# Attention and two MoE layers on one core: engine orders from block 6 on, staged weight preparation, weight loads at the turn

## The chip, the cores and the metric

The kernel runs on one core of one Trainium2 chip. The metric is the device time of one execution in microseconds (us). Before the change the median of three runs is 1075.56 us.

## The reference, cut to what matters

```python
def _attn_ref(q, k, v, f):                       # 4 batches, 8 heads, 576 tokens, head size 64
    cum = np.cumsum(np.log(np.clip(f, 0.0001, 1.0)), axis=-1)
    scores = q @ k.transpose(0, 1, 3, 2) / np.sqrt(64) + cum[:, :, :, None] - cum[:, :, None, :]
    ...                                          # causal mask, softmax
    return attn @ v

def reference(...):                              # x: 2304 tokens x 512
    h = np.maximum(x @ w_in, 0.0)                # first MoE layer, 512 -> 2048
    x = h * h @ w_out                            # 2048 -> 512
    h = x @ w_in2                                # second MoE layer
    return (h - np.tanh(h)) @ w_out2
```

All matmuls keep close to float32 exactness: each operand is held as a rounded half ("hi", h) and a rest ("lo", l), and a product is three matmuls: hi x hi, lo x hi, hi x lo. The weights of the second layer, w2, come as 64-bit numbers.

## The kernel before

**Blocks 0 to 7.** The first layer goes over 8 blocks of 288 tokens (TB), each in 16 steps i. `h_step` makes 12 matmuls (L157) into the one PSUM bank "h"; ScalarE makes ReLU (L161), the rounded square gh (L162) and the square (L163) from it, and VectorE the rest gl = square - gh (L117, the helper `rest`). `y_step` of the same step comes two steps later (LAG = 2): 12 matmuls (L173), of which those with gl need VectorE. The next h step can only start when ReLU has read the bank. The attention of the tokens lies beside blocks 0 to 5.

**Preparation for the second layer.** It lies beside blocks 6 and 7. w2 is cut in 8 pieces g for each half s (s = 0: w_in2, s = 1: w_out2); nine are prepared here: (0, 0) to (0, 7) and (1, 0). A piece means: `prep_fetch` reads raw 64-bit numbers; twice `prep_wide` (ScalarE, L765, tile wx), `prep_shift` (VectorE, L773) and `prep_or` (VectorE, L780) make 32-bit floats in tile wt; four `prep_sum` (VectorE, L785) build the sums of weights that a Strassen-like product of 7 factors needs; four casts `prep_hi` (ScalarE, L104) and four rests `prep_lo` (GpSimd, L117) split them; `prep_store` writes the piece to memory, and `w_load` reads it again when its place is free. Pieces in the table DIRECT are made in place instead. `PREPS` says after which (block, step) a piece is issued. The inputs x of the second layer are prepared in the same way for each of four quarters of the tokens: `x_load`, four sums `x_sum` (VectorE, L866), and `x_op` (cast on ScalarE L104, rest on GpSimd L117).

**Second part.** 32 steps n: quarter b, piece g. Each has 7 products of 6 matmuls (L969): P6, P1, P7 and P5 of step n, then P2, P4 and P3 of step n - 1, in a ring of 7 PSUM banks. ScalarE copies (L1103, L1108) and VectorE sums (L1104, L1107, L1120, L1121) combine them; tanh (L975) and the subtractions (VectorE L976, GpSimd L1132) give g = h - tanh(h), which `h_store` (L981) writes to g_d. Beside these steps the x operands of the next quarter and the pieces (1, 1) to (1, 7) are prepared (`PREP2_AT`: first step of a piece, which then takes four steps).

**The turn and the last part.** The last part has 32 product steps of 42 matmuls with 256 columns (L1045) and 192 matmuls more in `y_rest` (L1057). Its operands: `y_load` reads a g tile (L1008), `y_sum` makes four sums (VectorE, L1020), `y_hi` casts (ScalarE L104, tile go) and `y_lo` makes the rest (VectorE L117, tile go). Its weights are read by `w_load` into the places of w_in2 as those come free (`YLOAD_AT`, `HOME_G`); all DMAs go through the one queue of SyncE (SP), in order. "The turn" is the stretch around the last steps of the second part and the first of the last part.

**What sets the order.** The program is built twice. Up to step MARK, (2, 0), each engine follows the order of the first build. From there to the end of block 7 a scheduler that simulates a timeline orders the instructions. From the point where `second_part` is noted, before the change behind `part1.close()`, each engine's order is that in which the code emits its instructions:

```python
    for chain in ([by_name[n] for n in order if n in first_part], [x for x in emitted if x.name not in second_part]):
```

## Time and profile before

| | |
|---|---|
| median of three runs | 1075.56 us (1072.48 to 1077.96) |
| profiled execution, whole | 1073.96 us |
| its span | 1072.2 us |
| mean granted clock of TensorE | 0.987 |
| TensorE busy | 994.2 us, 93% |
| VectorE busy | 756.4 us, 71% |
| ScalarE busy | 586.1 us, 55% |
| GpSimd busy | 405.5 us, 38% |

The profile is of one execution. Its span goes from the first to the last instruction and is 1.76 us shorter than that execution's device time. Engines: PE is TensorE's matmuls, DVE is VectorE, ACT is ScalarE, POOL is GpSimd, SP is SyncE. L157 is line 157 of the kernel. "out<-in" are the program's names of tiles, "x12" a number of instructions. A wait is shown as the idle time of an engine with what ended it. Chain means the chain of work that ended last, followed back from the last instruction.

### The profile page before, as it was taken

The page shows a single profiled execution, that of the slowest core. Times are in us where ns is not written, and L with a number is a line of the kernel's source. Part 1 is how long each engine was busy: PE and PEld are TensorE (multiplying, and loading weights), DVE is VectorE, ACT ScalarE, POOL GpSimd, SP SyncE. Part 2 cuts the span into 40 slices and gives each one's busy share as a digit, 9 for nine tenths or more (in the row PEclk, how much of TensorE's full clock was granted, in tenths as well). Part 3 has the DMA queues.
Part 4 walks back from the last instruction along what each step waited for, and adds up shares of the span by engine and source line. Part 5 has one row for each costly group of instructions (what it writes and reads, how often), then busy time and mean ns, then how long its engine had stood idle before and what let it go on. Part 6 is the DMA issues. An engine that isn't in the chain of part 4 may idle for free.

```text
span 1072.2 us, 19736 instructions
## 1 busy us (share of the span) xinstructions
PE 994.2 (93%) x7008; PEld 925.1 (86%) x7008; DVE 756.4 (71%) x1843; ACT 586.1 (55%) x1314; POOL 405.5 (38%) x484
## 2 busy tenths in 40 slices
PE   4989999999999898998989998999999979999998
PEld 3676678888888788887889998999999979999998
DVE  5897777777777686787523766468877778777761
ACT  6887777765555455454435675446565644333330
POOL 4254455564454443543211556127576440000000
PEclk9899999999999999899999999999999999999999
DMA  7667642225864657744534994696867697335352
GB/s 239 196 151 206 193 141 98 89 86 174 273 196 158 191 176 219 251 130 132 194 120 145 318 335 141 224 417 230 320 244 269 259 346 266 135 98 175 121 163 74
DMA packets 86738, 211.55 MB, mean 197 GB/s; under 512 B 8592, under 2 KB 33232, under 8 KB 84336
## 3 DMA queue, kind: packets, MB, share of 16 engines
q1 hardware_dynamic: 86640, 210.29, 59.4%
q8 instruction: 55, 0.90, 0.3%
q14 instruction: 43, 0.35, 0.1%
HBM read 132.21 MB, written 78.05 MB: 196 GB/s over the span
## 4 chain that ended last, share of the span: by engine, by line
PE 58%; DMA 16%; DVE 14%; ACT 4%; issue 4%; POOL 2%; SPq 2%; POOLq 0%; DVEq 0%; ACTq 0%
PE wp L1045 15%; PE wp L969 13%; PE hp L157 9%; PE yp L173 8%; DMA PTl<-p_d 7%; PE o_ps L559 3%; DMA raw<-in_w_dram 3%; DMA p_d<-T 2%; PE wp L1057 2%; DVE PTl L117 2%; PE o_ps L374 2%; SPq L525 1%; DMA R<-in_qk_dram 1%; DVE P L450 1%; DVE gl L117 1%
## 5 line engine op out<-in xcount | busy, mean ns | idle before, releaser
L157 PE MATMUL hp<-xhl,w 128*128 128x288 f32 x1536 | 238.2, 301 | 7.1 <-ACT tmp L161 6.2
L157 PEld LDWEIGHTS hp<-xhl,w 128*128 128x128 f32 x1536 | 216.9, 192 | 13.6 <-ACT tmp L161 8.0
L173 PE MATMUL yp<-gh,w 128*128 128x288 f32 x1024 | 183.7, 299 | 0.5 <-ACT tmp L161 0.5
L969 PE MATMUL wp<-xo,wg 128*128 128x288 f32 x1152 | 162.4, 298 | 6.5 <-DMA wg<-wg_d 2.4
L1045 PE MATMUL wp<-go,wg 128*128 128x256 f32 x1344 | 162.7, 283 | 4.3 <-DVE go L117 3.3
L1045 PEld LDWEIGHTS wp<-go,wg 128*128 128x128 f32 x1344 | 161.7, 192 | 5.3 <-DVE go L117 4.1
L969 PEld LDWEIGHTS wp<-xo,wg 128*128 128x128 f32 x1152 | 156.9, 190 | 8.7 <-DVE gq L976 2.9
L173 PEld LDWEIGHTS yp<-gh,w 128*128 128x128 f32 x1024 | 153.9, 190 | 1.9 <-ACT tmp L161 0.7
L173 PE MATMUL yp<-gl,w 128*128 128x288 f32 x512 | 116.7, 301 | 12.1 <-DVE gl L117 9.3
L161 ACT ACTIVATE tmp<-hp 128x288 f32<-128x288 f32 x128 | 51.8, 405 | 123.8 <-PE hp L157 118.9
L104 ACT ACTIVATE go<-gt 128x1792 fp32r<-128x1792 f32 (+1 forms) x34 | 58.3, 1717 | 108.0 <-PE wp L1045 62.0
L459 ACT ACTIVATE P<-P,ST 128x320 f32<-128x320 f32 (+4 forms) x151 | 84.5, 561 | 43.1 <-DVE ST L450 42.2
L117 DVE TENSOR_TENSOR gl<-tmp,gh 128x288 fp32r<-128x288 f32 x96 | 58.4, 608 | 62.7 <-ACT tmp L163 62.3
L173 PEld LDWEIGHTS yp<-gl,w 128*128 128x128 f32 x512 | 84.0, 189 | 16.8 <-DVE gl L117 13.1
L470 POOL TENSOR_SCALAR P<-P,ST 128x448 f32<-128x448 f32 (+4 forms) x88 | 59.3, 676 | 96.9 <-DVE ST L464 54.8
L117 DVE TENSOR_TENSOR go<-gt,go 128x1792 fp32r<-128x1792 f32 (+1 forms) x34 | 69.3, 2038 | 27.6 <-ACT go L104 24.3
L117 POOL TENSOR_TENSOR wt<-wt,whi 128x512 f32<-128x512 f32 (+1 forms) x48 | 63.9, 1352 | 61.3 <-ACT whi L104 50.4
L117 DVE TENSOR_TENSOR PTl<-PTl,PTh 128x512 fp32r<-128x512 f32 (+1 forms) x64 | 51.7, 839 | 41.3 <-POOL PTh L106 41.3
L450 DVE CUSTOM_DVE_ANT_0 P<-s_ps,mk 128x320 f32<-128x320 f32 (+3 forms) x151 | 63.2, 433 | 25.1 <-PE s_ps L484 14.8
L106 POOL TENSOR_SCALAR PTh<-PTl 128x512 fp32r<-128x512 f32 (+1 forms) x64 | 46.1, 747 | 51.8 <-DMA PTl<-p_d 51.7
L1132 POOL TENSOR_TENSOR gq<-sm,sm 128x288 f32<-128x288 f32 x31 | 26.9, 868 | 94.1 <-ACT sm L1131 87.3
L1020 DVE TENSOR_TENSOR gt<-gt 128x256 f32<-128x256 f32 x128 | 53.4, 458 | 9.4 <-DMA gt<-g_d 8.3
(158 smaller groups left out, 1771.8 us busy)
## 6 DMA issues: line engine op xcount, KB each, us to landing
raw<-in_w_dram SPq DMA_DIRECT2D x64, 512.0 KB
wg<-wg_d SPq DMA_DIRECT2D x24, 896.0 KB
g_d<-gq SPq DMA_DIRECT2D x32, 576.0 KB
p_d<-T SPq DMA_DIRECT2D x16, 1024.0 KB
PTl<-p_d SPq DMA_DIRECT2D x64, 256.0 KB
gt<-g_d SPq DMA_DIRECT2D x32, 512.0 KB
R<-in_qk_dram SPq DMA_DIRECT2D x24, 576.0 KB
xhl<-x_d SPq DMA_DIRECT2D x14, 576.0 KB
```

Of the source, the lines that this page charges most:

```text
L104: eng.activation(out, in_, AF.Copy)
L106: eng.tensor_scalar(out, in_, 1.0, 1.0, ALU.mult, ALU.mult)
L117: eng.tensor_tensor(out, in_, hi.bitcast(F32), ALU.subtract)
L157: nc.tensor.matmul(ps, w[:, k * 128:(k + 1) * 128], x[:, k], start=(jj == 0), stop=(jj == 11))
L161: nc.scalar.activation(tmp, ps, AF.Relu)
L173: nc.tensor.matmul(yp[m][:, :n], w[:, c], x, start=(at == 0 and j == 0), stop=(at == NF - 1 and j == 2))
L450: nc.vector.tensor_tensor_reduce(p[:rows, a:b], ps[:rows, :b - a], mk[:rows, o:o + b - a], -0.125, 3.0e38 if mn is None else mn, ALU.add, ...
L459: nc.scalar.activation(p[:rows, :n], p[:rows, :n], AF.Exp, bias=mn, scale=-1.0, accum_out=st[:rows, 1, t:t + 1])
L470: by(n_by).tensor_scalar(p[:rows, :n], p[:rows, :n], st[:rows, 3, t:t + 1], 1.0, ALU.mult, ALU.mult)
L969: nc.tensor.matmul(ps, wg[:, ws, k * 128:(k + 1) * 128], xo[:, xs, k], start=(i == 0 and first_), stop=(i == 5), skip_group_check=True)
L1020: nc.vector.tensor_tensor(o, x, y, ALU.subtract)
L1045: nc.tensor.matmul(ps, wg[:, ws, m * 128:(m + 1) * 128], YO[n][xs][:, YX[xn]], start=(j == 0 and m == 0 and i == 0), stop=(j == 2 and i == ...
```

## The change

Four things are changed. (1) `second_part` is noted at the start of block 6, so that in blocks 6 and 7 too each engine follows the order of emission. (2) In these blocks a piece of w2 starts every third step (`PREPS` now counts the 32 steps of blocks 6 and 7) and is done in steps of its own: wide, shifts and ORs in the first, four sums and half of the casts and rests in the second, the other half in the third, the stores in the fourth (`prep_step`, `beside`); raw numbers are fetched two pieces ahead into two buffers; sums and operands of x stand at fixed steps (`XSUM_AT`, `XOP0_AT`); x of block 7 is read at step 8 of block 6 instead of 13. (3) In the second part three x sums stand in step 5 of a quarter and one in step 7, the pieces of w_out2 take the steps of `PREP2` (the last two earlier than before), and of the weights of the last part two pieces are loaded behind steps 27 and 30 and four behind the first four product steps, with `HOME_G` changed to suit. (4) At the turn g tiles are read behind other steps (`YGT_AT`), `y_sum(0)` stands a step earlier, `y_lo(0)` too, `y_hi(1)` ahead of the last P2; at the end the second half of `y_rest` finishes one output half before it starts the other.

```diff
-PREPS = (((6, 1), 0, 0), ((6, 3), 0, 1), ((6, 6), 0, 2), ((6, 8), 0, 3), ((6, 11), 0, 4), ((6, 13), 0, 5),
-         ((7, 1), 1, 0), ((7, 6), 0, 6), ((7, 10), 0, 7))
-PREP2_AT = (None, 2, 6, 10, 14, 18, 25, 28)
-DIRECT = {(0, 6): 0, (0, 7): 1, (1, 6): 4, (1, 7): 6}
-HOME_G = ({6: 0, 7: 1, 0: 2, 1: 3, 2: 4, 3: 5, 4: 6, 5: 7}, {0: 2, 1: 3, 6: 4, 2: 5, 7: 6, 3: 7, 4: 0, 5: 1})
+PREPS = ((1, 0, 0), (4, 0, 1), (7, 0, 2), (10, 0, 3), (13, 0, 4), (16, 0, 5), (19, 1, 0), (22, 0, 6), (25, 0, 7))
+XSUM_AT = {25: ("T1", "T3"), 26: ("T2",), 28: ("T4",)}
+XOP0_AT = {26: ("B11",), 28: ("T1", "T3"), 29: ("T2",), 30: ("B21", "T4"), 31: ("B22",)}
+PREP2 = {1: (2, 3, 4, 4, 5), 2: (6, 7, 8, 8, 9), 3: (10, 11, 12, 12, 13), 4: (14, 15, 16, 16, 17), 5: (18, 19, 20, 20, 21),
+         6: (22, 23, 24, 25, 26), 7: (26, 27, 28, 28, 29)}
+DIRECT = ((0, 6), (0, 7), (1, 6), (1, 7))
+HOME_G = ({6: 0, 7: 1, 0: 2, 1: 3, 2: 4, 3: 5, 4: 6, 5: 7}, {6: 2, 7: 3, 0: 4, 1: 5, 2: 6, 3: 7, 4: 0, 5: 1})
...
-    def prep_all(s, g):
-        with tc.issue_after(latest(EngineType.DVE)):
...
+    def prep_step(k, n):
+        s, g = PREPS[k][1:]
+        if n == 0:
+            for m in range(2):
+                prep_wide(s, g, m)
+            for m in range(2):
+                prep_shift(s, g, m)
+                prep_or(s, g, m)
+            if k + 2 < len(PREPS):
+                prep_fetch(*PREPS[k + 2][1:], ("raw", "sm0")[k % 2])
+            elif k + 1 == len(PREPS):
+                prep_fetch(1, 1)
+        elif n == 1:
+            for x in ("S1", "S3", "S2", "S4"):
+                prep_sum(s, g, x)
+            for a, b in ((1 - s, 2), (2, 4)):
+                prep_hi(s, g, a, b)
+                prep_lo(s, g, a, b)
+        elif n == 2:
+            for a, b in ((4, 6), (6, 8)):
+                prep_hi(s, g, a, b)
+                prep_lo(s, g, a, b)
+        elif (s, g) not in DIRECT:
             for which in range(2):
                 prep_store(s, g, which, 1 - s, 8)
+
+    def beside(it):
+        for n in (3, 2, 0, 1):
+            for k in range(len(PREPS)):
+                if it - PREPS[k][0] == n:
+                    prep_step(k, n)
+        for at, f in ((XSUM_AT, x_sum), (XOP0_AT, x_op)):
+            if it in at:
+                f(0, at[it])
...
-                prep_fetch(*PREPS[0][1:])
+                for k in range(2):
+                    prep_fetch(*PREPS[k][1:], ("raw", "sm0")[k])
+                second_part = {x.name for x in nc.cur_bb.bb.instructions}
...
+            if j >= NB - 2:
+                beside(g - (NB - 2) * NF)
...
-            for k, (at, *which) in enumerate(PREPS):
-                if (j, i) == at:
-                    prep_all(*which)
-                    prep_fetch(*(PREPS[k + 1][1:] if k + 1 < len(PREPS) else (1, 1)))
...
-            if i == XLOAD and j + 1 < NB:
+            if i == (8 if j == NB - 2 else XLOAD) and j + 1 < NB:
                 X[j + 1] = load_x(j + 1)
...
             if iy == 3:
                 x_load(0)
-                x_sum(0, ("T1", "T2", "T3", "T4"))
-            elif iy == 7:
-                x_op(0, ("T2", "B11", "T3", "T1", "B21", "T4", "B22"))
-            else:
+            elif iy == 11:
                 w_load(0, 0)
                 w_load(0, 1)
...
-    second_part = {x.name for x in nc.cur_bb.bb.instructions}
...
-    XOP_AT = {4: ("B11",), 6: ("T2",), 7: ("B21",)}
-    TSUM_AT = {4: ("T1", "T3"), 5: ("T2", "T4")}
-    YLOAD_AT = {25: 0, 26: 1, 28: 2, 30: 3, 31: 4}
+    XOP_AT = {5: ("B11",), 6: ("T2",), 7: ("B21",)}
+    TSUM_AT = {5: ("T1", "T2", "T3"), 7: ("T4",)}
+    YLOAD_AT, YLOAD2_AT = {27: 0, 30: 1}, {0: 2, 1: 3, 2: 4, 3: 5}
+    YGT_AT = {26: 0, 27: 1, 29: 2}
...
-        active = [(n - PREP2_AT[k], k) for k in range(1, NG) if 0 <= n - PREP2_AT[k] < 4]
-
+        active = [(i, k) for k in PREP2 for i in range(5) if PREP2[k][i] == n]
...
-            elif stage == 2:
+            elif stage == 3:
                 prep_hi(1, k, 0, 4)
                 prep_lo(1, k, 0, 2)
                 prep_lo(1, k, 2, 4)
-            elif stage == 3:
+            elif stage == 4:
                 prep_hi(1, k, 4, 8)
...
+        if n == NSTEP - 3:
+            y_sum(0)
         if n == NSTEP - 2:
-            y_sum(0)
             y_hi(0)
+            y_lo(0)
         if n == NSTEP - 1:
-            y_lo(0)
             y_sum(1)
...
     n = NSTEP - 1
+    y_hi(1)
     GQ[n] = late.tile([128, 4, N2], F32, tag="gq", bufs=2, name="gq")
...
-    y_hi(1)
     y_lo(1)
...
-        if n == 1:
-            w_load(1, 5)
+        if n in YLOAD2_AT:
+            w_load(1, YLOAD2_AT[n])
...
-    for u in range(2):
-        y_rest(u, acc)
+    parts = ((1, ("A11", "A12")), (0, ("A21", "A22")))
+    y_rest(0, acc, parts)
+    for part in parts:
+        y_rest(1, acc, (part,))
```

In the changed kernel the lines are shifted by 2 (L117 is L119, L161 is L163), by 7 (L773 is L780) or by some 20 to 30 (L866 is L893, L976 is L999, L1104 is L1125).

VectorE in block 7, around the preparation of piece (1, 0) (gl: rest of a step; wt: weights; xa: x operands), before:

```order
L117 TENSOR_TENSOR gl<-tmp,gh 128x288 x3
L866 TENSOR_TENSOR xa<-xa 128x576
L117 TENSOR_TENSOR gl<-tmp,gh 128x288
L773 TENSOR_SCALAR wt<-raw 128x512 x2
L780 SCALAR_TENSOR_TENSOR wt<-wx,wt 128x512
L866 TENSOR_TENSOR xa<-xa 128x576 x2
L785 TENSOR_TENSOR wt<-wt 128x256
L866 TENSOR_TENSOR xa<-xa 128x576
L780 SCALAR_TENSOR_TENSOR wt<-wx,wt 128x512
L117 TENSOR_TENSOR gl<-tmp,gh 128x288
L785 TENSOR_TENSOR wt<-wt 128x256 x3
```

and after:

```order
L119 TENSOR_TENSOR gl<-tmp,gh 128x288 x2
L780 TENSOR_SCALAR wt<-raw 128x512
L787 SCALAR_TENSOR_TENSOR wt<-wx,wt 128x512
L780 TENSOR_SCALAR wt<-raw 128x512
L787 SCALAR_TENSOR_TENSOR wt<-wx,wt 128x512
L893 TENSOR_TENSOR xa<-xa 128x576 x2
L119 TENSOR_TENSOR gl<-tmp,gh 128x288
L792 TENSOR_TENSOR wt<-wt 128x256 x4
L893 TENSOR_TENSOR xa<-xa 128x576
L119 TENSOR_TENSOR gl<-tmp,gh 128x288 x2
L893 TENSOR_TENSOR xa<-xa 128x576
L119 TENSOR_TENSOR gl<-tmp,gh 128x288 x4
```

Before, up to eight instructions of the preparation stand ahead of one gl; now shifts and ORs of a piece stand together, with the x sums of the same step, and the four sums stand behind the next gl.

ScalarE around the first piece (tmp, gh: an h step's activations; wx: the wide cast; whi: the cast of weights; yst: output of a block), before, in block 5:

```order
L161 ACTIVATE tmp<-hp 128x288
L162 ACTIVATE gh<-tmp 128x288
L163 ACTIVATE tmp<-tmp 128x288
L765 ACTIVATE wx<-raw 128x512
L161 ACTIVATE tmp<-hp 128x288
L162 ACTIVATE gh<-tmp 128x288
L163 ACTIVATE tmp<-tmp 128x288
```

and after, in block 6:

```order
L163 ACTIVATE tmp<-hp 128x288
L164 ACTIVATE gh<-tmp 128x288
L165 ACTIVATE tmp<-tmp 128x288
L772 ACTIVATE wx<-raw 128x512 x2
L163 ACTIVATE tmp<-hp 128x288
L164 ACTIVATE gh<-tmp 128x288
L165 ACTIVATE tmp<-tmp 128x288
L711 ACTIVATE yst<-yp 128x288 x2
L106 ACTIVATE whi<-wt 128x256
L106 ACTIVATE whi<-wt 128x512
```

The scheduler took a wide cast into block 5; now both stand together behind the first step of block 6, with the casts of the first half a step later.

VectorE at the turn (sm, wp: sums of products; gq: g; gt: sums of a g tile; go: its rest), before:

```order
L976 TENSOR_TENSOR gq<-wp,sm_8292 128x288 x3
L1020 TENSOR_TENSOR gt<-gt 128x256 x4
L1104 TENSOR_TENSOR sm_8291<-wp,sm_8291 128x288
L1107 TENSOR_TENSOR wp<-wp,sm_8291 128x288
L1120 TENSOR_TENSOR sm_8291<-wp,sm_8291 128x288
L1121 TENSOR_TENSOR wp<-wp,sm_8291 128x288
L976 TENSOR_TENSOR gq<-wp,sm_8292 128x288 x3
L117 TENSOR_TENSOR go<-gt,go 128x1792
L1020 TENSOR_TENSOR gt<-gt 128x256 x4
L976 TENSOR_TENSOR gq<-wp,sm_8292 128x288 x3
L117 TENSOR_TENSOR go<-gt,go 128x1792
L1020 TENSOR_TENSOR gt<-gt 128x256 x4
```

and after:

```order
L999 TENSOR_TENSOR gq<-wp,sm_8283 128x288 x3
L1043 TENSOR_TENSOR gt<-gt 128x256 x4
L1125 TENSOR_TENSOR sm_8282<-wp,sm_8282 128x288
L1128 TENSOR_TENSOR wp<-wp,sm_8282 128x288
L1141 TENSOR_TENSOR sm_8282<-wp,sm_8282 128x288
L1142 TENSOR_TENSOR wp<-wp,sm_8282 128x288
L999 TENSOR_TENSOR gq<-wp,sm_8283 128x288 x3
L119 TENSOR_TENSOR go<-gt,go 128x1792
L1125 TENSOR_TENSOR sm_8282<-wp,sm_8282 128x288
L1128 TENSOR_TENSOR wp<-wp,sm_8282 128x288
L1141 TENSOR_TENSOR sm_8282<-wp,sm_8282 128x288
L1142 TENSOR_TENSOR wp<-wp,sm_8282 128x288
```

The first tile's sums stand a step earlier, and its rest (go) ahead of the last step's sums and not behind them.

## Rows read from the trace of the kernel before

**Rows 1.** The page, part 1: busy time of the engines.

```profile
PE 994.2 (93%) x7008; PEld 925.1 (86%) x7008; DVE 756.4 (71%) x1843; ACT 586.1 (55%) x1314; POOL 405.5 (38%) x484
```

**Rows 2.** Stages from:to us: length, busy PE, PEld, DVE, ACT, POOL (instructions), granted clock, DMA, GB/s.

```profile
555.30:690.86 135.56, 125.37 (x918) 123.15 (x917) 75.82 (x120) 79.75 (x178) 55.88 (x43) 0.99 0.66 229
690.86:748.47 57.61, 54.36 (x388) 52.97 (x387) 42.10 (x85) 29.24 (x70) 25.11 (x21) 0.97 0.84 321
...
848.47:872.84 24.37, 22.76 (x171) 22.45 (x169) 17.76 (x36) 12.12 (x28) 11.88 (x12) 1.00 1.02 395
872.84:888.61 15.77, 9.84 (x71) 8.68 (x69) 12.24 (x18) 7.52 (x13) 6.01 (x4) 1.00 0.87 304
```

**Rows 3.** The chain that ended last, from 600 us: start us, us, what.

```profile
638.74 1.59 PE yp L173 x12
640.33 1.59 PE hp L157 x12
...
747.31 102.13 PE wp L969 x764
...
899.17 146.17 PE wp L1045 x1216
```

**Rows 4.** Groups by line and shape, 555.30 to 690.86 us.

```profile
L157 PE MATMUL hp<-xhl,w 128*128 128x288 f32 x444 | 66.2, 299 | 3.1 <-ACT tmp L161 3.0
...
L117 POOL TENSOR_TENSOR wt<-wt,whi 128x512 f32<-128x512 f32 x22 | 29.6, 1374 | 16.2 <-DVE wt L785 10.9 <-ACT whi L104 5.4
L117 DVE TENSOR_TENSOR gl<-tmp,gh 128x288 fp32r<-128x288 f32 x38 | 28.6, 752 | 50.9 <-ACT tmp L163 50.9
...
L785 DVE TENSOR_TENSOR wt<-wt 128x256 f32<-128x256 f32 x36 | 19.6, 561 | 0.7
...
L161 ACT ACTIVATE tmp<-hp 128x288 f32<-128x288 f32 x37 | 15.0, 405 | 29.1 <-PE hp L157 29.0
L780 DVE SCALAR_TENSOR_TENSOR wt<-wx,wt 128x512 uint32<-128x512 uint32 x18 | 14.2, 790 | 3.6 <-ACT wx L765 3.2
...
L773 DVE TENSOR_SCALAR wt<-raw 128x512 uint32<-128x512 uint32 x18 | 11.6, 669 | 0.0
```

**Rows 5.** Waits of TensorE, 555.30 to 690.86 us: us in total, times, longest.

```profile
PE yp L173 <- DVE gl L117: 7.1, 5, 3.4
```

**Rows 6.** Timeline of VectorE, block 7: start us, us, instruction [idle before].

```profile
650.06 1.99 DVE L773 TENSOR_SCALAR wt<-raw 128x512 uint32<-128x512 uint32 x2
...
658.86 3.51 DVE L785 TENSOR_TENSOR wt<-wt 128x256 f32<-128x256 f32 x3
...
670.03 0.75 DVE L773 TENSOR_SCALAR wt<-raw 128x512 uint32<-128x512 uint32 x2
```

**Rows 7.** Timeline of ScalarE at three places.

```profile
559.12 0.66 ACT L765 ACTIVATE wx<-raw 128x512 f32<-128x512 f32 x1 [3.85 <-DMA raw<-in_w_dram]
...
661.94 0.63 ACT L104 ACTIVATE wg<-wt 128x512 fp32r<-128x512 f32 x1 [3.03 <-DVE wt L785]
...
884.80 1.70 ACT L104 ACTIVATE go<-gt 128x1792 fp32r<-128x1792 f32 x1 [4.95 <-POOL gq L1179]
```

**Rows 8.** Timeline of TensorE, third step of the second part.

```profile
700.36 6.17 PE L969 MATMUL wp<-xo,wg 128*128 128x288 f32 x34 [2.41 <-DMA wg<-wg_d]
```

**Rows 9.** The chain at the turn to the last part.

```profile
850.49 12.84 DMA g_d<-gq
...
886.53 2.04 DVE go L117
```

**Rows 10.** Timeline of VectorE, second part and turn.

```profile
725.84 3.58 DVE L866 TENSOR_TENSOR xa<-xa 128x576 f32<-128x576 f32 x2
...
869.12 3.78 DVE L1020 TENSOR_TENSOR gt<-gt 128x256 f32<-128x256 f32 x4
...
880.29 4.35 DVE L1020 TENSOR_TENSOR gt<-gt 128x256 f32<-128x256 f32 x4
...
888.47 1.55 DVE L1020 TENSOR_TENSOR gt<-gt 128x256 f32<-128x256 f32 x4
```

More of the change, by code (lines that the diff above doesn't have):

```diff
@@ L751, in place, with prep_fetch @@
         WG[s, g] = {k: hl[:, :, i - 1] for k, i in (SLOT[s] | SUMS).items() if i}
-    def prep_fetch(s, g):
-        raw = WRAW[s, g] = late.tile([128, 2, 1024], U32 if WIDE else F32, tag="raw", name="raw")
+    def prep_fetch(s, g, tag="raw"):
+        raw = WRAW[s, g] = late.tile([128, 2, 1024], U32 if WIDE else F32, tag=tag, name="raw")
         for n, a in enumerate(((1, 0), (0, 1))[s]):
@@ L762, in prep_wide @@
         if WIDE:
-            x = WX[s, g, n] = (pa[1] if s and g else late).tile([128, 512], F32, tag="x" if s and g else "sm1", name="wx")
+            if s and g:
+                x = WX[s, g, n] = pa[1].tile([128, 512], F32, tag="x", name="wx")
+            else:
+                if n == 0:
+                    WX[s, g] = late.tile([128, 2, 512], F32, tag="sm1", name="wx")
+                x = WX[s, g, n] = WX[s, g][:, n]
             raw = WRAW[s, g][:, n].rearrange("p (n c) -> p n c", c=2)
@@ L1136 @@
             h_act(n - 1, 2)
-        if b + 1 < B and g in XOP_AT:
-            x_op(b + 1, XOP_AT[g])
         if g == 0 and b:
@@ L1142 @@
             x_sum(b + 1, TSUM_AT[g])
+        if b + 1 < B and g in XOP_AT:
+            x_op(b + 1, XOP_AT[g])
         for stage, k in active:
@@ L1166 @@
         for stage, k in active:
-            if stage >= 2:
-                a = 4 * (stage - 2)
+            if stage >= 3:
+                a = 4 * (stage - 3)
                 for which in range(2):
```

19 lines of the change are left out of this document (5 added, 14 removed).

## Prediction

> **What bounds the kernel now.** I read the profile in this order: busy time of the engines, busy time by stage, the chain of waits and TensorE's timeline for the pace of each stage, and then, where a stage is longer than its pace, the timelines of VectorE, ScalarE and the weight-load transfers.
>
> TensorE is busy for 93% of the span [rows 1], so it is the bound, and what an edit can give back is the time in which it doesn't run at its pace. The change leaves the instructions up to the last steps of block 5 where they were, so I look from 555.30 us on. The paces come from runs of the chain without a wait [rows 3]: 12 matmuls of an h step take 1.59 us and 12 of a y step 1.59, so a step of blocks 0 to 7 takes 3.18; a matmul of the second part takes 102.13 / 764 = 0.1337 us, so a step of 42 takes 5.61; a matmul of the last part takes 146.17 / 1216 = 0.1202. Against these, stage by stage [rows 2] (the counts in the rows take in a few matmuls that straddle an edge):
>
> - End of block 5 to the end of block 7: 444 matmuls of line 157 are 37 steps [rows 4]; with two y steps more and the 16 matmuls of the second part that stand ahead of the last y step (16 x 0.1337 = 2.1) the pace gives 37 x 3.18 + 2 x 1.59 + 2.1 = 122.9 us. The stage took 135.56: **12.6 us lost**.
> - The first ten steps of the second part: 386 matmuls follow, 51.6 us; it took 57.61: **6.0 lost**.
> - 848.47 to 872.84: four steps, 22.4; it took 24.37: **1.9 lost**.
> - The turn from the second part to the last, 872.84 to 888.61: 24 matmuls of 0.1337 and 44 of 0.1202 are 8.5 us; it took 15.77: **7.3 lost**. Behind it some 0.5 more.
>
> Together 28.3 us from block 5's end on. Whatever the change gives comes out of these.
>
> **The change, part by part.** *Orders of blocks 6 and 7, and preparation in stages.* In the losses of this stretch TensorE mostly waits for gl of VectorE, 7.1 us in 5 waits [rows 5]; the time lost is more than the waits, as the matmuls behind a wait restart slowly. What makes gl late is the order: at 650 us the scheduler put two shifts, three x sums, two ORs and a sum ahead of one gl, and they met GpSimd's work: two shifts took 1.99 us there and 0.75 where GpSimd stood still, three sums 3.51 [rows 6]. ScalarE, in order too, stood 3.03 us before a cast of weights that waited for those sums, with Square and ReLU queued behind it [rows 7], and the next h step waits for that ReLU. Block 5 loses time in the same way: a cast of weights sits in ScalarE's queue ahead of its ReLU and waited 3.85 us for its raw weights [rows 7].
>
> In the changed order a piece takes three steps, 9.54 us: shifts and ORs in the first, four sums and half of the casts in the second, the rest of the casts in the third. VectorE's load in a period, by the means of the stretch [rows 4]: 3 gl x 0.752 + 4 sums x 0.561 + 2 ORs x 0.790 + 2 shifts x 0.669 = 7.4 of 9.54. The lateness that a gl can bear is two steps, 6.4 us, since y(i) stands behind h(i+2); a first step with all shifts and ORs ahead of its gl delays it by 2 x 0.669 + 2 x 0.790 = 2.9. So gl holds nothing up. For ReLU the casts of the third step must not be late: they need the four sums (2.2 us), which start when gl of the first step is done, some 2 us after its h step; counted from that h step's end they are done at about 4.5, when ScalarE, through with the next step's three activations of some 0.4 us each [rows 4], gets to the casts (3.18 + 1.3); two of 0.63 [rows 7] end at 5.8, and the ReLU of that step is due at 6.4. It fits with 0.5 us to spare, and TensorE's y step of 1.59, less 0.4 for ReLU itself, gives 1.2 more. Raw weights are now fetched two pieces, 19 us, ahead into two buffers, so no cast waits for them, and the first cast stands in step 1 of block 6. By this the stretch loses nothing; as some sums will meet GpSimd, I take 2 us, with 0 as one end and a late ReLU in each of 9 periods, 9 x 1.2 = 11, as the other. That gl comes after two matmuls in the new y step and not after eight costs nothing while gl is early. Extra DMAs: none; x of block 7 is read five steps earlier into buffers that are free by then.
>
> *Start of the second part.* TensorE stands 2.41 us for weights of the third step, and the 34 matmuls behind take 6.17 us where the pace gives 4.5 [rows 8]: the granted clock averages 0.97 in that stretch [rows 2]. Those weights are loaded behind the last y step, and the 16 matmuls that were taken ahead of it shorten the cover by 2.1 us. Now all 68 matmuls that come first stand behind it, 9.1 us, and the load landed 700.36 - 690.86 = 9.5 us after that y step's end. I take a wait of 0.4, between 0 and 2, and of the 6.0 lost the 3.9 that the wait and the slow restart made are gone but for that.
>
> *x sums in one step.* The other 2.1 us were lost where x sums met GpSimd (two took 3.58 us) [rows 10] and held up the subtractions that free TensorE's banks. The change puts three of them into step 5 of each quarter, later than the x load, with the casts and GpSimd beside them. At 1.79 us each [rows 10] three are 5.4; at 1.55 for four of under half the size [rows 10], some 2.6. In the later quarters, inside the chain's 102 us without a wait [rows 3], two sums in one step stopped nothing; one more sum is at most 1.8 us more. I take 0.5 us in each of three quarters, 1.5, between 0 and 2.7 (0.9 each). Preparation of weights 6 and 7, moved three steps ahead, now lies beside the last quarter's x operands, as that of weights 4 did inside the same 102 us: nothing.
>
> *Weight loads spread.* At 850 us the chain is a store of g, 12.84 us [rows 9], behind two weight loads and two g loads in one queue; VectorE waited for it before it could write the next g. With loads behind steps 27 and 30 alone, and four in the last part, at most one load lies ahead of a store: the 1.9 us go. The load for the fifth product step of the last part is issued behind the first one's matmuls, four steps of 42 x 0.1202 = 5.05 us ahead, so nothing is late there. On SP's queue it stands behind g loads that wait for a rest of g, which VectorE has done by then.
>
> *The turn.* Before, the sums of the first g tile took 3.78 us and those of the second 4.35, against 1.55 alone [rows 10], as GpSimd was on the last weights; the casts of g waited for them, 4.95 us in the worst case [rows 7, 10]. Weights 7 are now done by step 29, the first sums stand in step 29, cast and rest (1.70 and 2.04 us) [rows 7, 9] in step 30, the second sums in 31 and their cast ahead of the last tanh. I walked the in-order queues from step 29: the first sums still meet GpSimd's last two pieces. With 2.95 us for them (midway between 1.55 and 4.35), the rest in step 30 makes step 31's chain about 2 us late; then TensorE waits 0.4 before P4 of step 31, 0.8 and 0.15 in the first product step for the last banks, 1.75 for the second g tile, whose rest is queued behind three subtractions, and 0.2 and 0.25 for the next two: 3.6 us against 7.8. With 1.55 it is 2.9, with 4.35 it is 5.0. The Trainium skill (SBUF — State Buffer, "SBUF: two separate sides") says that VectorE with two SBUF inputs and a GpSimd instruction that reads SBUF lock each other out for a whole instruction; by that rule each of the first sums that comes second waits out a GpSimd piece, and the turn would cost the 5.0. The trace agrees in kind [rows 6, 10]; in amount its rows lie on both sides.
>
> *The end.* The last part's two halves finish one behind the other, so that one eviction and its store lie under matmuls; the other half still ends the kernel. I take 0.
>
> Sum: 28.3 lost before, 2 + 0.4 + 1.5 + 3.6 = 7.5 after, so 20.8 us less. The profiled execution took 1073.96 us in all (span 1072.2), which gives 1053.2; the median of the three runs is 1.6 higher, which gives 1054.8. I say **1054**.
>
> **The rivals.**
> 1. *Stalls move in blocks 6 and 7.* A fixed order can't slip: ReLU queues behind casts that queue behind sums on another engine. If each of the 9 pieces delays ReLU by the 1.2 us of the bound, 11 us stay lost there, 9 more than taken, and the time is 1063 or, with the upper ends of the x sums and the turn (1.2 and 1.4 more), 1065.6. For it: the queues are ordered just so, and GpSimd works 3 x 1.374 us and a half piece more in each period [rows 4]. Against: 0.5 + 1.2 us to spare. Chance 0.16.
> 2. *The change doesn't do at the turn what it says*: the sums meet GpSimd a step earlier instead, and a second wait for g stays. The turn keeps 6 to 7.8 us, 2.4 to 4.2 more than taken: 1056 to 1058. Chance 0.12.
> 3. *VectorE becomes the bound, slower than before.* If the four sums beside GpSimd put all its work into the long form: 2 shifts 1.99, 4 sums 4.7 (3.51 for three), 2 ORs and 3 gl in proportion (twice their means) 3.2 and 4.5: 14.4 us in a period of 9.54, 4.9 x 9 = 44 us lost, 1073.96 - 28.3 + 44 + 5 = 1095. It decides where the mean is 28% over that of the stretch (9.54 / 7.4) [rows 4], and makes the kernel slower than before from about 12 us in a period. Against: GpSimd has only 5 us of work in a period. The rule of the Trainium skill's SBUF — State Buffer page on the shared port pair is this mechanism; the trace bears it out for single instructions, not for whole periods. Chance 0.04.
> 4. *Nothing to measure*: the 11 us of rival 1, the turn's 7.8 and x sums that cost 5 leave 24 of the 28.3, some 1070 to 1075. Chance 0.05.
>
> **How the numbers follow.** The forecast (1048.5 to 1056) has 0.63. No change means within 0.5%, 5.4 us, about what a measurement of this kernel can tell. Faster by more than that: forecast, rivals 1 and 2, 0.91; same 0.05; slower 0.04. The range takes the bounds of the unknown costs: 2.9 us lost after the change and nothing else gives 1073.96 - 25.4 = 1048.5; rival 1 with its ends 1065.5.
>
> **What would show it.** Right: h steps at 3.18 us through blocks 6 and 7 and no wait for gl over 1 us; no wait for weights in the third step of the second part; stores of g that land within one step; waits of TensorE at the turn of 3 to 5 us, the largest for the second g tile. Wrong: TensorE waiting for h_step's ReLU again and again in steps 2 and 3 of the pieces; VectorE near 100% in blocks 6 and 7; or the same waits for g at the turn.

## The result, and the profile after

The changed kernel takes **1067.55 us** (median of ten runs, 1063.4 to 1073.63) against 1076.76 for the one before (ten runs, 1072.48 to 1080.39): a ratio of 0.9917, interval 0.989 to 0.9945. That is 9.2 us less where 20.8 were forecast, and above the range's upper end of 1065.5. The profiled execution took 1069.37 us, its span is 1067.6.

The first part of the span, in which nothing was changed, is not the same in two executions: step 11 of block 5 begins at 555.3 us in the trace of before and at 559.6 in that of after (in the twelve traces of this case, one of each kernel, it lies between 552.6 and 559.6). So I compare from that step on. Each boundary below is the start of the same matmul in each trace, counted within its line on TensorE's timeline; a length is the difference of two such starts. "Pace" is the count of matmuls by the rate without a wait: 37 steps of 3.18 us and two y steps of 1.59 in A, 11.20 us for two steps of 42 in the second part and 10.08 in the last, as both traces show them where nothing waits.

| stage | pace | before | after | predicted for after |
|---|---|---|---|---|
| A: block 5 step 11 to the last matmul of the last y step | 120.8 | 135.43 | 120.73 | 122.8 |
| B: to step 6 of the second part | 31.2 | 33.23 | 32.49 | 31.6 |
| C: steps 6 to 30 | 134.4 | 136.60 | 145.47 | 135.9 |
| D: step 30 to product step 2 of the last part | 23.7 | 32.93 | 26.21 | 27.3 |
| E: product steps 2 to 10 | 40.3 | 40.81 | 45.20 | 40.3 |
| F: the rest | | 137.87 | 137.88 | 137.87 |
| together | | 516.87 | 507.98 | 495.8 |

The 8.9 us that the table gives agree with the 9.2 of the medians. The 16 matmuls of the second part that stood ahead of the last y step before, 2.1 us, lie in stage A there and in B after; so against the pace A lost 12.5 us before and B 4.1. A and D came out as forecast or better, C and E lost 9.6 and 4.9 us that the forecast did not have.

The page's engines and the busy time of the five stages, after (columns as in [rows 1] and [rows 2]):

```profile
PE 1001.6 (94%) x7008; PEld 931.4 (87%) x7008; DVE 755.7 (71%) x1843; ACT 586.7 (55%) x1314; POOL 403.4 (38%) x484
```

```profile
559.60:680.47 120.87, 120.24 (x903) 119.78 (x902) 72.98 (x120) 81.30 (x177) 55.31 (x43) 1.00 0.71 253
680.47:712.82 32.35, 31.42 (x236) 31.18 (x235) 18.92 (x45) 14.73 (x35) 6.32 (x6) 1.00 1.01 391
712.82:858.29 145.47, 139.76 (x1010) 136.16 (x1009) 116.85 (x230) 83.02 (x191) 87.77 (x72) 0.99 0.68 248
858.29:884.50 26.21, 24.76 (x188) 23.84 (x187) 19.64 (x34) 11.58 (x21) 5.41 (x6) 1.00 0.66 232
884.50:929.70 45.20, 42.04 (x338) 40.69 (x337) 33.42 (x52) 15.68 (x10) 0.00 (x0) 1.00 0.73 280
```

In the first stage TensorE is busy for 120.24 of 120.87 us where it stood and restarted before [rows 2]; the waits for gl [rows 5] are gone, and one wait of 0.5 us for ReLU is left. In stage B the wait for weights of the third step is shorter:

```profile
690.60 4.78 PE L992 MATMUL wp<-xo,wg 128*128 128x288 f32 x34 [0.93 <-DMA wg<-wg_d]
```

In stage C TensorE is busy for 139.76 of 145.47 us, and VectorE for 116.85. What VectorE did there, at the start of the loss in the first quarter, and what TensorE waited for (timelines: start, us, instruction, idle before and what ended it):

```profile
714.55 1.19 DVE L999 TENSOR_TENSOR gq<-wp,sm 128x288 f32<-128x288 f32 x3 [2.70 <-DMA g_d<-gq]
715.66 5.25 DVE L893 TENSOR_TENSOR xa<-xa 128x576 f32<-128x576 f32 x3
720.84 0.45 DVE L1125 TENSOR_TENSOR sm<-wp,sm 128x288 f32<-128x288 f32 x1
```

```profile
716.75 3.54 POOL L119 TENSOR_TENSOR wt<-wt,whi 128x512 f32<-128x512 f32 x2
```

```profile
721.34 6.54 PE L992 MATMUL wp<-xo,wg 128*128 128x288 f32 x36 [2.03 <-DVE sm L1125]
```

Three x sums take 5.25 us, nearly a whole step of 5.6, with GpSimd's rests beside them; L1125 of the next step, which reads a bank of TensorE, is queued behind them, and TensorE stands 2.03 us. In this first quarter VectorE also waited 2.70 us for a store of g ahead of the sums, as the first row shows. Of the 11.1 us that stage C loses against its pace, 5.4 lie in steps 6 to 10 and 2.8 in each of the two later quarters (steps 14 to 16 take 12.54 us and 16 to 18 take 12.70, where the pace is 11.20). In the second quarter the sums, a shift (L780), the fourth sum and the weight sums follow one another on VectorE, which does not stand still for as much as 0.2 us from the first of these rows to past the last:

```profile
764.13 4.42 DVE L893 TENSOR_TENSOR xa<-xa 128x576 f32<-128x576 f32 x3
...
772.53 1.70 DVE L780 TENSOR_SCALAR wt<-raw 128x512 uint32<-128x512 uint32 x1
...
777.89 1.19 DVE L893 TENSOR_TENSOR xa<-xa 128x576 f32<-128x576 f32 x1
779.01 1.98 DVE L792 TENSOR_TENSOR wt<-wt 128x256 f32<-128x256 f32 x2
```

In stage E it is the g tiles. VectorE, and the chain of waits (start, us, what):

```profile
897.03 1.55 DVE L1043 TENSOR_TENSOR gt<-gt 128x256 f32<-128x256 f32 x4 [2.23 <-DMA gt<-g_d]
...
903.98 1.55 DVE L1043 TENSOR_TENSOR gt<-gt 128x256 f32<-128x256 f32 x4 [3.46 <-DMA gt<-g_d]
```

```profile
881.79 9.49 DMA gt<-g_d
...
894.83 14.80 DMA gt<-g_d
```

and SyncE's queue, where each read of a g tile (L1031, 512 KB) stands behind a weight load of two reads (L869, 896 KB each):

```profile
882.43 1.08 SPq L869 DMA_DIRECT2D wg<-wg_d  x2
884.84 0.53 SPq L1031 DMA_DIRECT2D gt<-g_d  x1
885.48 1.12 SPq L869 DMA_DIRECT2D wg<-wg_d  x2
890.15 0.53 SPq L1031 DMA_DIRECT2D gt<-g_d  x1
```

At the turn, VectorE's first g sums still met GpSimd (3.62 us), the second ones no longer (1.55), and the two waits of TensorE behind the first 30 matmuls of the last part are 0.41 and 0.99 us:

```profile
859.37 3.62 DVE L1043 TENSOR_TENSOR gt<-gt 128x256 f32<-128x256 f32 x4
...
872.56 1.55 DVE L1043 TENSOR_TENSOR gt<-gt 128x256 f32<-128x256 f32 x4
```

```profile
876.68 1.94 PE L1068 MATMUL wp<-go,wg 128*128 128x256 f32 x14 [0.41 <-DVE gq L999]
879.61 2.66 PE L1068 MATMUL wp<-go,wg 128*128 128x256 f32 x20 [0.99 <-DVE go L119]
```

### The profile page after: what moved, and what is told of

The parts are those of the page before. It is cut to its first block, busy times and chain, and to the rows that moved or that the text cites. A ratio compares the mean times of both kernels' runs of the same rounds, so it can differ in the third digit from the quotient of the medians.

```text
span 1067.6 us, 19745 instructions
## 1 busy us (share of the span) xinstructions
PE 1001.6 (94%) x7008; PEld 931.4 (87%) x7008; DVE 755.7 (71%) x1843; ACT 586.7 (55%) x1314; POOL 403.4 (38%) x484
## 4 chain that ended last, share of the span: by engine, by line
PE 55%; DVE 17%; DMA 17%; issue 3%; ACT 3%; SPq 2%; POOL 2%; POOLq 0%; DVEq 0%; ACTq 0%
PE wp L1068 11%; PE hp L159 11%; PE yp L175 11%; PE wp L992 9%; DMA PTl<-p_d 7%; PE o_ps L561 3%; DMA p_d<-T 3%; DMA gt<-g_d 2%; PE wp L1080 2%; DMA g_d<-gq 2%; PE o_ps L376 2%; DVE PTl L119 2%; DVE xa L893 2%; DVE P L452 2%; SPq L527 1%
## 5 line engine op out<-in xcount | busy, mean ns | idle before, releaser
L175 PE MATMUL yp<-gh,w 128*128 128x288 f32 x1024 | 198.2, 300 | 0.0
L175 PEld LDWEIGHTS yp<-gh,w 128*128 128x128 f32 x1024 | 160.5, 191 | 1.2 <-issue 0.4
L175 PE MATMUL yp<-gl,w 128*128 128x288 f32 x512 | 133.4, 302 | 4.8 <-DVE gl L119 3.0
L163 ACT ACTIVATE tmp<-hp 128x288 f32<-128x288 f32 x128 | 51.9, 406 | 133.8 <-PE hp L159 115.3
L119 DVE TENSOR_TENSOR gl<-tmp,gh 128x288 fp32r<-128x288 f32 x96 | 58.6, 611 | 60.5 <-ACT tmp L165 60.0
L175 PEld LDWEIGHTS yp<-gl,w 128*128 128x128 f32 x512 | 91.0, 192 | 8.0 <-DVE gl L119 4.5
L119 DVE TENSOR_TENSOR go<-gt,go 128x1792 fp32r<-128x1792 f32 (+1 forms) x34 | 69.3, 2038 | 23.5 <-ACT go L106 20.5
L119 POOL TENSOR_TENSOR wt<-wt,whi 128x512 f32<-128x512 f32 (+1 forms) x48 | 62.5, 1323 | 61.0 <-DVE wt L792 36.3
L119 DVE TENSOR_TENSOR PTl<-PTl,PTh 128x512 fp32r<-128x512 f32 (+1 forms) x64 | 51.7, 840 | 41.5 <-POOL PTh L108 41.5
L1043 DVE TENSOR_TENSOR gt<-gt 128x256 f32<-128x256 f32 x128 | 50.5, 437 | 17.7 <-DMA gt<-g_d 16.6
```

What stands on the lines that cost most here:

```text
L119: eng.tensor_tensor(out, in_, hi.bitcast(F32), ALU.subtract)
L163: nc.scalar.activation(tmp, ps, AF.Relu)
L175: nc.tensor.matmul(yp[m][:, :n], w[:, c], x, start=(at == 0 and j == 0), stop=(at == NF - 1 and j == 2))
L1043: nc.vector.tensor_tensor(o, x, y, ALU.subtract)
```

## The experiments

Lengths are by the stages of the table, from the same matmuls, in the one trace of each kernel.

**x sums two and two.**

```diff
-    XOP_AT = {5: ("B11",), 6: ("T2",), 7: ("B21",)}
-    TSUM_AT = {5: ("T1", "T2", "T3"), 7: ("T4",)}
+    XOP_AT = {4: ("B11",), 6: ("T2",), 7: ("B21",)}
+    TSUM_AT = {4: ("T1", "T3"), 5: ("T2", "T4")}
```

> The changed kernel with the x sums of a quarter put back to two in step 4 and two in step 5 (and B11 back to step 4); all else as changed. In the changed kernel's trace the second part loses 11.1 us against its pace in steps 5 to 8 of the three quarters (4.5 + 0.9, 2.8, 2.8), and VectorE shows three sums of 5.25 us in one run with the sums that free TensorE's banks queued behind them. Theory A (the run of three sums is longer than the slack of one step): the loss falls to the 2 us that the kernel before had there, so about 9 us less than the changed kernel's 1067.6, 1058.5, and TensorE's wait for line 1125 goes. Rival B (the staged rests and casts of GpSimd and ScalarE beside the sums, or the order of x sums and x operands in the code, cost it, wherever the sums stand): at least 7 of the 11.1 stay, 1064 or more. Rival C (late stores of g at the start of the second part): the first quarter keeps its 5.4, the others gain, 1062.

1059.45 us (five runs), ratio to before 0.9846 (0.9804 to 0.9888). Stage C falls from 145.47 to 139.24, and the two later quarters lose 0.65 and 0.62 us where the changed kernel loses 2.8 each. Theory A holds for these two quarters. The whole gain of stage C is 6.2 us where 9 were expected: in the first quarter 3.6 of the 5.4 us stay, which is nearer to rival C, and their cause stays open. They are not the x sums' place alone, as these stand where they stood before, when 2.1 were lost there.

**GpSimd quiet beside three sums.**

```diff
-    XOP_AT = {5: ("B11",), 6: ("T2",), 7: ("B21",)}
+    XOP_AT = {4: ("B11",), 6: ("T2",), 7: ("B21",)}
...
-                prep_lo(1, k, 4, 6)
-                prep_lo(1, k, 6, 8)
+                if k not in (1, 3, 5):
+                    prep_lo(1, k, 4, 6)
+                    prep_lo(1, k, 6, 8)
```

> The changed kernel, three sums still in step 5 of a quarter, but without GpSimd's work beside them: the operand B11 is made in step 4, and the rests of the second half of the weight pieces 1, 3 and 5 (two GpSimd instructions in step 5, 13 and 21) are left out, so the output is not the reference's. If the length of the sums by GpSimd's work is the cause (theory A1), three sums take 3 x 0.76 = 2.3 us and the loss of steps 5 and 6 goes: 8 to 9 us less than the changed kernel, about 1059. If three sums in a run are too many in any case, as they stand ahead of the sums that free the banks (theory A2), at least 1.5 us stay lost in each quarter there, and the time is 1062 or more.

The kernel leaves out the two rests of pieces 1, 3 and 5 that would lie beside the sums. 1056.49 us (two runs), stage C 138.40, 7.1 less than in the changed kernel. In the two later quarters three sums in one step cost nothing in the steps behind them when GpSimd is quiet; VectorE's timeline in the second quarter, with the shift and the fourth sum that follow:

```profile
756.98 2.21 DVE L893 TENSOR_TENSOR xa<-xa 128x576 f32<-128x576 f32 x3
...
763.17 1.71 DVE L780 TENSOR_SCALAR wt<-raw 128x512 uint32<-128x512 uint32 x1
...
768.53 1.19 DVE L893 TENSOR_TENSOR xa<-xa 128x576 f32<-128x576 f32 x1
769.64 1.98 DVE L792 TENSOR_TENSOR wt<-wt 128x256 f32<-128x256 f32 x2
```

2.21 us against 5.25 and, in the same quarter of the changed kernel, 4.42; steps 14 to 16 are back at the pace (11.20). So theory A1: neither three in a row nor their place alone, but their length beside GpSimd's work. The fourth sum still stands in step 7 here, and in this quarter the shift, the fourth sum and the weight sums take as long as in the changed kernel; yet steps 16 to 18 lose 0.63 us and 24 to 26 lose 0.45, where the changed kernel loses 1.5 in either. So some 0.9 to 1.0 of the 1.5 was lateness passed on from the three sums. In the first quarter 2.9 us stay lost with GpSimd quiet.

**g tiles read ahead of the weights.**

```diff
         if n == NSTEP - 1:
             y_sum(1)
+            y_load(4)
...
     y_load(3)
+    y_load(5)
...
-        y_load(n + 4)
         if n in YLOAD2_AT:
...
             y_lo(2)
+            y_load(6)
...
             y_lo(n + 2)
+            y_load(n + 6)
```

> The changed kernel with the reads of g tiles 4 and later issued earlier: tile 4 in step 31 of the second part, 5 behind the rest of tile 1, and n + 6 behind the rest of tile n + 2, so that each stands in SyncE's queue ahead of weight loads that come before it now. In the changed kernel TensorE loses 4.4 us in product steps 5 to 9 of the last part, VectorE waits four times for a g tile (1.2 to 3.5 us), and the chain goes over two g loads of 9.5 and 14.8 us. Theory D (g loads queued behind the four weight loads, 1.8 MB each, in a stretch where the DMA engines are 100% busy at about 400 GB/s): the g waits go, the weights, needed four steps later, still come in time, and the last part loses nothing from step 4 on: 1067.6 - 4.4 = 1063. Rival E (the stretch is short of DMA bandwidth whatever the order): the wait moves from g to weights, TensorE waits for wg of line 869 instead, and less than 1.5 us are gained. Rival F (earlier g loads delay the stores of g at steps 30 and 31): 1 to 3 us lost at the turn.

1064.49 us (five runs), ratio 0.9902 (0.9867 to 0.9938). Stage E takes 41.79 in place of 45.20, stage D 26.20: theory D, with 1 us left of the 4.4, and nothing of rival F. Rival E is refuted, as TensorE waits for no weights there, and by the busy time of the first four product steps of stage E, in which TensorE is never short of work although the DMA engines are full (1.02, 409 GB/s):

```profile
883.04:903.71 20.67, 20.65 (x170) 20.27 (x169) 16.49 (x29) 8.41 (x5) 0.00 (x0) 1.00 1.02 409
```

**Blocks 6 and 7 alone.** From the changed kernel, the second part, the turn and the end were put back: x sums two and two, `PREP2` 6 and 7 at (25, 26, 27, 27, 28) and (28, 29, 30, 30, 31), and

```diff
-    YLOAD_AT, YLOAD2_AT = {27: 0, 30: 1}, {0: 2, 1: 3, 2: 4, 3: 5}
-    YGT_AT = {26: 0, 27: 1, 29: 2}
+    YLOAD_AT, YLOAD2_AT = {25: 0, 26: 1, 28: 2, 30: 3, 31: 4}, {1: 5}
+    YGT_AT = {26: 0, 27: 1, 30: 2}
```

with `HOME_G`, `y_sum(0)`, `y_lo(0)`, `y_hi(1)` and the order of `y_rest` as before.

> The changed kernel with its second part, turn and end as before (sums two and two, weight loads, their places, g loads, first g sums, last pieces and rest order as before); what stays of the change is the orders and the staged preparation of blocks 6 and 7 and the start of the second part. In the traces, blocks 6 and 7 lose 0.9 us against their pace, 11 us less than before, and the start of the second part 1.2 against 4.1. Theory: 28.3 us were lost before from block 5's end on, and some 14 of them go with this part alone: 1076.8 - 14 = 1063. Rival: the gain of blocks 6 and 7 is chance of one profile, or falls to later waits (the second part then waits for its weights): 1070 or more.

1056.92 us (five runs), ratio 0.9847 (0.9801 to 0.9893). From step 11 of block 5 on it takes 502.10 us, 14.8 less than before, as worked out (some 14): 14.7 in stage A, of which 2.1 are the matmuls that now lie in B, 0.4 in B, C within 0.4, D and E as before. The median fell by 18.8; the stages account for 14.8 of it. So this part alone is worth more than the whole change; the remaining parts together cost 5.9 us (507.98 against 502.10).

**Both mended terms.** The edits of the first and third experiment together.

> The two mended terms together: x sums two in step 4 and two in step 5, and g tiles read ahead of the weight loads. If the two losses are independent, the gains add: from step 11 of block 5 to the end the kernel before took 516.9 us, the changed one 508.0, the first edit alone 501.4, the second alone 504.5, so both 501.4 - 3.5 = 497.9, 19 us less than before; as a median 1075.8 - 19 = 1057 or, from the medians of the two runs, 1059.5 - 3.1 = 1056. Rival: with the sums gone the g loads meet stores earlier and a wait for g or for weights comes back at the turn: 500 or more from block 5 on, 1059 or more. It should also beat the kernel with the staging alone (502.1 from block 5 on) by 4 us, which is what the turn is then worth.

**1053.43 us** (six runs), ratio 0.9819 (0.978 to 0.9857). From step 11 of block 5 on 497.84 us, where 497.9 were worked out: the two losses are independent. Stage E takes 41.79 us as with the second edit alone, B and C together 171.2 as with the first; that the sums meet within 0.1 is luck, as stage B alone differs by up to 1.4 us between kernels with the same order in it (31.61 to 33.04). It is 4.3 us less than with blocks 6 and 7 alone, where 4 were expected. It is the fastest kernel of this study by its median, 14 us under the changed one, of which the stages account for 10.1.

**Spread loads alone, and loads in a row.** The first is the kernel with blocks 6 and 7 alone, plus the changed `YLOAD_AT`, `YLOAD2_AT` and `HOME_G`. The second is the changed kernel with sums two and two and

```diff
-    YLOAD_AT, YLOAD2_AT = {27: 0, 30: 1}, {0: 2, 1: 3, 2: 4, 3: 5}
+    YLOAD_AT, YLOAD2_AT = {27: 0, 28: 1, 29: 2, 30: 3, 31: 4}, {1: 5}
```

> The kernel with the staging alone, plus the weight loads of the last part as changed (two behind steps 27 and 30, four behind the first four product steps, with their new places); the last pieces, the g loads, sums, casts and rests of the turn stay as before. From step 30 of the second part to product step 2 of the last, before and staging alone take 32.9 us, the changed kernel 26.2. Theory G (the moved sums, casts and rests and the earlier last pieces give the turn; the spread loads give at most the 1.9 us that stores of g waited): 31 to 33 us here. Theory H (the loads held up the stores, and so the whole turn): 26 to 28. In either case the product steps 4 to 10 lose about 4 us to g loads behind weight loads, which staging alone does not, if that loss comes from the spread loads.

> The complement: the changed turn (earlier last pieces, moved sums, casts and rests; x sums two and two), but the weight loads of the last part behind steps 27, 28, 29, 30 and 31 and one behind the second product step, nearly as densely as before. Theory G: the turn stays at 26 to 28 us, since it is the moved sums, and the last part loses nothing in product steps 4 to 10. Theory H: the stores of g wait for the loads again, and the turn is back at 31 us or more. As g is written later by these waits, a wait of VectorE for a store in steps 28 to 31 of over 2 us would show it.

Spread loads alone: 1062.22 us (two runs), stage D 31.05, stage E 44.38. Loads in a row with the moved sums: 1056.2 us (two runs), D 26.23, E 45.06. So the moved sums, casts and rests, with the earlier last pieces, gave the turn (theory G): 6.7 us with them in either arrangement of loads, 1.9 with the spread loads alone. Which of the moved sums and the earlier pieces gave how much was not tried. The wait of VectorE for a store in steps 28 to 31, the sign named for theory H, is absent with loads in a row (before, the longest was 2.69). And the spread loads cost 3.6 us in stage E without any other edit of the turn. The second expectation held to the letter alone: product steps 4 to 10 lose nothing, but with loads in a row stage E did lose 4.25 us, only earlier, in product steps 2 to 4, as g tiles 3 and 4 (counted from 0) then stood behind the loads. VectorE there:

```profile
875.53 3.02 DVE L1043 TENSOR_TENSOR gt<-gt 128x256 f32<-128x256 f32 x8 [2.68 <-DMA gt<-g_d]
```

**Shifts together.**

```diff
                 prep_shift(1, k, 0)
+                prep_shift(1, k, 1)
...
                 prep_wide(1, k, 1)
-                prep_shift(1, k, 1)
```

> The kernel with both mended terms, and the second shift of a weight piece in the second part moved ahead, next to the first one. With the sums two and two, 0.65 us each stayed lost in steps 6 to 8 of the second and third quarter, where the kernel with the staging alone loses nothing though every engine has the same order there: in the one the second shift begins with GpSimd's rest of an x operand (768.20 and 768.19 us) and takes 1.72 us, in the other (765.13 and 765.12) 0.42. Theory: which of the two gets ahead decides, and a shift that does not stand there cannot lose; then both 0.65 go, 1.3 us less than with both terms alone and up to 2 with the first quarter. Rival: another instruction of VectorE (the sums of weights, an OR) takes its place in the same way, and the 0.65 stay or grow.

1055.8 us (six runs), ratio 0.9822 (0.9793 to 0.9851); from step 11 of block 5 on 497.40, 0.4 less than with both mended terms: stage C 1.2 less, stage B 0.8 more, so nothing that can be told from chance. The 0.65 us of steps 16 to 18 are gone (11.21), but steps 14 to 16 now take 11.68: the rival has it, most of the loss moved by two steps. It is an OR that takes the shift's place: the first one takes 1.21 us here beside GpSimd's work and 0.68 with the sums two and two, and TensorE then waits 0.23 us for the subtraction behind it.

**A piece in one step.** `prep_step` does sums, casts and rests in the piece's first step, for the seven pieces not made in place.

```diff
-        elif n == 1:
+        if n == ((s, g) in DIRECT):
             for x in ("S1", "S3", "S2", "S4"):
...
-        elif n == 2:
+        if n == 2 * ((s, g) in DIRECT):
...
```

> The kernel with both mended terms, but seven of the nine weight pieces of blocks 6 and 7 issued in one step each (wide, shifts, ORs, sums, casts and rests together; the two that are made in place keep their steps); engine orders fixed as in the changed kernel. It asks what gave blocks 6 and 7 their pace: the fixed order alone or the stages. Theory: the stages. In one step the casts of a piece stand ahead of the step's ReLU and wait for 2 x 0.67 + 2 x 0.79 + 4 x 0.56 = 5.2 us of VectorE behind the gl of the step before, so ReLU is some 7 us behind that h step's end where 3.2 are to be had, and TensorE loses 3 to 4 us a piece: 20 to 28 us in all from step 11 of block 5 to the last y step, 141 to 149 us in place of 120.7, and 1074 to 1081 for the whole. Rival: the fixed order alone keeps the pace (at most 5 us lost, 126).

1081.77 us (three runs), ratio 1.0065 (1.0015 to 1.0116). Stage A takes 149.78 us, 29.05 more than with stages, a little above the 20 to 28. The waits of TensorE in blocks 6 and 7 (us in total, times, longest), and ScalarE's queue in front of one ReLU (L163):

```profile
PE hp L159 <- ACT tmp L163: 17.0, 8, 2.5
```

```profile
592.16 1.15 ACT L106 ACTIVATE whi<-wt 128x512 fp32r<-128x512 f32 x2 [0.90 <-DVE wt L792]
593.21 0.39 ACT L163 ACTIVATE tmp<-hp 128x288 f32<-128x288 f32 x1
```

Without the stages each of the seven pieces costs some 4 us more than with them, and this fixed order is slower in stage A than the scheduler's, by 14.4 us (149.78 against 135.43).

**One raw buffer.**

```diff
-            if k + 2 < len(PREPS):
-                prep_fetch(*PREPS[k + 2][1:], ("raw", "sm0")[k % 2])
+            if k + 1 < len(PREPS):
+                prep_fetch(*PREPS[k + 1][1:], "raw")
...
-                for k in range(2):
-                    prep_fetch(*PREPS[k][1:], ("raw", "sm0")[k])
+                prep_fetch(*PREPS[0][1:], "raw")
```

> The kernel with both mended terms, but raw weights fetched one piece ahead into one buffer, as before the change, in place of two pieces ahead into two. Theory: it costs nothing now, as the fetch is issued behind the ORs of the first step and a piece comes every 9.5 us, of which some 6 remain for the transfer: 120.7 us from step 11 of block 5 to the last y step, within 1. Rival: the earlier fetch is what took the waits of ScalarE for raw weights away (3.85 us at one place before), and without it each of the 8 later pieces delays ReLU by 1 to 3 us: 129 or more.

1057.89 us (two runs), stage A 124.1: 3.4 us lost, in block 7 alone. Neither side had it: most pieces lose nothing, and one waits long (waits of ScalarE in blocks 6 and 7):

```profile
ACT wx L772 <- DMA raw<-in_w_dram: 4.6, 3, 3.5
```

## Why the prediction was wrong, and where it was right

**Right: blocks 6 and 7.** The largest term, 12.6 us lost before and 2 after, came out as 0 after (stage A 120.73, pace 120.8). Its reason holds as well: within a fixed order it is the stages that keep gl and ReLU on time, since pieces in one step lose 29 us. Stages left to the scheduler were not tried. Rival 1 (ReLU queued behind casts) is just what that experiment shows, and what the staging avoids: TensorE waits 17.0 us for ReLU there and 0.5 in the changed kernel. Rival 3 did not happen: VectorE was busy for 72.98 of 120.87 us.

**Right: the turn.** 3.6 us were forecast lost after the change; stage D shows 2.5 against its pace. Of the waits named two were there, 0.41 and 0.99 us, the second, for the second g tile, smaller than the 1.75 worked out; ahead of P4 of step 31 the profile shows none. The first sums met GpSimd as forecast and took 3.62 us; the 5.0 us that the prediction worked out for sums of 4.35 us, and by the rule that it cites, did not come. The 1.9 us of the stores of g fit the 1.9 that the spread loads give alone, but beside the moved sums, casts, rests and pieces the spread adds nothing: the turn is as short with loads in a row.

**Right in kind: the start of the second part.** The wait of 2.41 us [rows 8] became 0.93; stage B lost 1.3 where 0.4 was taken, inside the bound of 2. In the ten kernels built from the changed one it lost from 0.4 to 1.8, so the one value says no more. The end, taken as 0, was 0 (stage F).

**Wrong: x sums in one step.** The step read: three sums 5.4 us beside GpSimd, "I take 0.5 us in each of three quarters, 1.5, between 0 and 2.7". The duration was right: 5.25 us. The price to TensorE was not: stage C lost 11.1 us, 9.6 more than taken. What failed is the overlap: the bound counted one extra sum (1.8 us) against an assumed slack, where VectorE's row of work in those steps has almost none. The sums of products, g's subtractions, the weight piece and 4.4 to 5.25 us of sums fill the steps of 5.6 us, and what is late is passed on to the next steps with their shifts and weight sums: 1.3 us are lost in steps 14 to 16 and 1.5 in 16 to 18, where 0.9 was the bound for both. The prediction had a sign of it: in its own account two sums beside GpSimd went with 2.1 us lost in the first quarter [rows 10], and it took 0.5 for three. The fourth sum, put into step 7 beside two weight sums, was not costed at all; no run prices it alone, but with the row on time no more than 0.63 and 0.45 us are lost around it. That GpSimd's work beside the three sums is the cause, not their number, is what the quiet experiment shows: 2.21 us, steps 14 to 16 at their pace, and 7.1 of the 11.1 us gone. The other 4.0 are those 0.63 and 0.45 and 2.9 in the first quarter, where late stores of g may have a part; that stays open. The Trainium skill's rule of the shared port pair (SBUF — State Buffer, "SBUF: two separate sides") is that a VectorE instruction with two SBUF inputs and a GpSimd instruction that reads SBUF exclude each other, and the one that starts second waits for the other's end. The trace agrees in kind, with 5.25 and 4.42 us beside GpSimd and 2.21 without.

**Wrong: weight loads spread.** The step read: "nothing is late there", worked out for the weights alone, which are needed four product steps later and did come in time. It looked at the g loads ahead of the weights in the queue and did not ask what stands behind them: a g tile that is read behind a product step is summed in the next one, 5 us later, and from the second product step on it sits behind the 1.8 MB of weights issued a step before. This cost 4.4 us (stage E), a term that the sum did not have; with the reads of g ahead of the loads 1.0. What a moved load pushes back in its queue was counted for the stores of g and not for the reads.

**The range** ended 2 us too low, since the x sums' upper bound was 2.7 us for a loss of 11.1 and the g reads had none. Put right, the two terms give back 10.1 us from step 11 of block 5 on (507.98 to 497.84, where the forecast amounts to 495.8), and the median of the kernel with both mended is 1053.43. That this lies so near to the 1054 of the forecast is in part luck: in its trace step 11 of block 5 begins at 552.6 us, 2.7 earlier than in the one that the forecast starts from.

## What to carry to other kernels

An in-order engine's work is costed per step against what that step has left, not per instruction: where it has no idle time left, 1 us too much in one step is paid in the following steps too. For a DMA that is moved, ask of every transfer behind it in the queue when it is needed, not only of the moved one; small reads with near deadlines go ahead of large ones with far deadlines, even where the DMA engines stay full. And split a large edit: one part of this one was worth 15 us, and two others took 10 of what it could have given.
